# One exponential of a period among its transposes, routing and projection moved by half a pair

## The chip, the cores and the metric

One program runs on one core of a Trainium2 chip. The metric is the device time of a run in microseconds (us). The kernel before took 787.89 us in the median of three runs (787.39 to 789.18). The engines have short names throughout: PE is TensorE (matmul), PEld its weight load, DVE is VectorE, ACT is ScalarE, POOL is GpSimd, and SP is SyncE, which here only issues transfers (DMAs).

## The reference, cut to what matters

Attention over 4 batches of 8 heads, 768 tokens and 64 features, in which a query sees a key only if the signs of their projections on 6 vectors agree; then a top-1 mixture of 8 experts on the 3072 tokens.

```python
q_bits = (np.einsum('bhsd,dk->bhsk', q, proj) > 0).astype(np.int64)
k_bits = (np.einsum('bhsd,dk->bhsk', k, proj) > 0).astype(np.int64)
...
mask = q_bucket[:, :, :, None] == k_bucket[:, :, None, :]
scores = scale * np.matmul(q, k.transpose(0, 1, 3, 2))
scores = np.where(mask, scores, -1000000000.0)
scores = scores - np.max(scores, axis=-1, keepdims=True)
attn = np.exp(scores)
attn = attn / (np.sum(attn, axis=-1, keepdims=True) + 1e-09)
return np.matmul(attn, v).astype(np.float32)
...
logits = x @ w_gate
e_idx = np.argmax(logits, axis=1)
...
eom = 1.0 / (1.0 + np.exp(-(x @ w_output_gate)))
for e in range(E):
    mask = e_idx == e
    h = np.maximum(x[mask] @ w1[e], 0.0)
    out[mask] = gate_w[mask, None] * eom[mask, e, None] * (h @ w2[e])
```

## The kernel before

The first half of the program (to about 465 us) is the attention. It runs over 16 pairs of heads. A pair has 12 steps, one for each 128 queries of each of its two heads; 192 steps in all. Six steps are a period (`PER`), half a pair. Step s does this:

- PE makes the scores of step s (`scores`, line 529): for each half of the keys two matmuls, one with the rounded operands `xl`, `xr` and one with the remainders and the mask rows, `yl`, `yr`. The result has two PSUM buffers (`ps_s`). DVE takes the row minimum while it copies them out (line 533); only then is the PSUM buffer free.
- ACT makes the exponential (`soft`, line 541), DVE the reciprocal of two steps' sums (lines 548 and 549), POOL multiplies (`normal`, line 551).
- PE transposes the weights of step s-6 (`transposed`, line 562), in two halves of three, and ACT copies each half out (line 563). These also have two PSUM buffers (`ps_t`).

At the first step of a period (k == 0) PE also does the weighted sums of the half pair that was transposed in the period before (`weighted`, line 573, 24 matmuls with `ps_a`), between its score and its transposes. That is when ACT has no copies to make, and four exponentials stand there; the other two stand behind the transposes of the third and fourth step (k 2 and 3).

In every second period, the one that begins at step 12(g-1), the operands of pair g are made. I call it the operand period. POOL rounds q and k (`split_hi`, line 487), DVE makes the remainders (`split_lo`, line 495, four halves), PE projects q and k on the 6 vectors (`project`, line 407, behind the weighted sums), DVE turns the signs into mask rows (`bt`, line 410), and SP sends it all to its places with 16 DMAs (`spread`, lines 504 to 512). One of them copies `xl` inside itself and so waits for those that read the same rows; two write mask rows into `yl` and wait for the copy that reads `yl`. q and k of pair g are loaded by SP (`load`, line 394).

The order on PE, DVE, ACT and POOL is the order in which the program is written: the loop over the steps, with tables of functions by step (`at`, `first`, `amid`, `ahead`, `narrow`, `last`). The order on SP is set by a scheduler from when it expects things to be ready; SP then issues strictly in that order, and one that waits holds up all behind it.

When a batch of 4 pairs is through, its tokens are routed, in small pieces spread over the next batch's steps (`routing`). Counted from the first step of the next batch they stand at: router products at 6 and 12, `tokens` 8 and 14, `best` 15, `choose` 19, `prefix` and `ranks` 20, `gate_sums` 21, `gate_values` and `places` 22, `columns` 24, `hot` 25, `table` (12 matmuls, line 226) 28, `entries` 29. Nearly all of them are small DVE instructions. With three of the four batches routed, the first expert is picked (`pick`), its tokens gathered and its weights loaded and split, while the attention of the last batch still runs.

The second half of the program is the experts' matmuls, one expert after the other.

The structure that the change touches is this, at k == 0:

```python
elif k == 0:
    for fn in first.get(s, ()):
        fn()
    normals()
    softs(2)
    ...
if s >= PER and k in (2, 3):
    softs(1)
```

Of the kernel before, what the change touches and what calls it, by code (L numbers as in the profile page):

```python
# [19 lines left out]
B, H, S, D = 4, 8, 768, 64  # L20
NB = 6
P = 128
NT = S // P
# [36 lines left out]
def lsh_attention_then_moe(  # L60
# [307 lines left out]
    with ExitStack() as actx:  # L368
# [11 lines left out]
        at, first, amid, ahead, narrow, last = {}, {}, {}, {}, {}, {}  # L380
# [4 lines left out]
        def plan(step, *fns):  # L385
            at.setdefault(step, []).extend(fns)

# [329 lines left out]
        for g in range(NP):  # L717
            s0 = 12 * (g - 1)
            if g >= 2:
                plan(s0 - 8, lambda g=g: load(g))  # L720
                first.setdefault(s0, []).extend(lambda g=g, j=j: split_hi(g, j) for j in range(2))
                amid.setdefault(s0, []).extend(lambda g=g, n=n: split_lo(g, 0, n) for n in range(2))
                ahead.setdefault(s0, []).extend(lambda g=g, n=n: split_lo(g, 1, n) for n in range(2))
                narrow.setdefault(s0, []).append(lambda g=g: project(g))
                last.setdefault(s0, []).extend(lambda g=g, j=j: spread(g, j) for j in range(2))
            elif g == 1:
                plan(4, lambda: project(1))
                for j in range(2):
                    plan(2 + j, lambda j=j: split_hi(1, j))
                    for n in range(2):  # L730
                        plan(3 + 2 * j + n, lambda j=j, n=n: split_lo(1, j, n))
                    plan(5 + j, lambda j=j: spread(1, j))
            if g >= 1:
                plan(s0 + 10, lambda g=g: load_v(g))
            for hf in range(2 if g + 1 < NP else 1):
                narrow.setdefault(12 * g + 6 * hf + 2 * PER, []).extend(
                    lambda hb=2 * g + hf, c=c: weighted(hb, c) for c in range(NT))
                if g + 1 < NP:
                    plan(12 * g + 6 * hf + 2 * PER, lambda g=g, hf=hf: rows(g, hf))
        for i, fn in enumerate(more_constants()):  # L740
            plan(18 + 2 * i, fn)
        for b in range(B - 1):
            r = routing(b)
            s0 = 12 * (H // 2) * (b + 1)
            for hf in range(2):
                narrow.setdefault(s0 + PER * (hf + 1), []).insert(0, lambda r=r, hf=hf: r["logits"](hf, H // 2))
            for n, fn in ((8, lambda r=r: r["tokens"](0, H // 2)), (14, lambda r=r: r["tokens"](1, H // 2)),
                          (15, r["best"]), (19, r["choose"]), (20, r["prefix"]), (20, r["ranks"]),
                          (21, r["gate_sums"]), (22, r["gate_values"]), (22, r["places"]), (24, r["columns"]),
                          (25, r["hot"]), (28, r["table"]), (29, r["entries"])):  # L750
                plan(12 * (H // 2) * (b + 1) + n, fn)
# [4 lines left out]
        for hf in range(2):  # L756
            narrow.setdefault(s0 + PER * (hf + 1), []).insert(0, lambda hf=hf: r["logits"](hf, lp))
# [4 lines left out]
        late = 12 * (H // 2) * (B - 1) + 23  # L762
# [83 lines left out]
        with tc.manual_schedule(engines=MANUAL):  # L846
# [30 lines left out]

            for s in range(NSTEP + LAG):
# [13 lines left out]
                elif k == 0:  # L892
                    for fn in first.get(s, ()):
                        fn()
                    normals()
                    softs(2)
                    normals()
                    for fn in amid.get(s, ()):
                        fn()
                    softs(2)  # L900
                    normals()
                    for when in (ahead, narrow, last):
                        for fn in when.get(s, ()):
                            fn()
# [4 lines left out]
                if s >= PER and k in (2, 3):  # L909
                    softs(1)  # L910
# [257 lines left out]
```

## Time and profile before

| what | value |
|---|---|
| median of three runs | 787.89 us (787.39 to 789.18) |
| the profiled execution, its own time | 785.37 us |
| its span from the first to the last instruction | 783.7 us |
| PE busy | 753.6 us, 96% |
| PEld busy | 608.5 us, 78% |
| DVE busy | 494.7 us, 63% |
| ACT busy | 459.2 us, 59% |
| POOL busy | 389.9 us, 50% |
| mean granted clock of PE | 0.990 |

The shares are means over two halves that differ much: DVE, ACT and POOL have most of their work in the attention, where a period of six steps is the unit to look at. Matmuls are pipelined and their ends are modelled, so two of them can overlap in a timeline; distances between starts say more than lengths. A granted clock of 1.00 is 2.4 GHz, 0.50 is 1.2 GHz.

### The profile page before, as it was taken

Reading aid. Unit: us, or ns where it says so; the run is one execution under the profiler, and the core shown is the slowest. Engines: PE = TensorE matmul, PEld = TensorE weight load, DVE = VectorE, ACT = ScalarE, POOL = GpSimd, SP = SyncE. Lnnn points to the kernel's source line nnn. Section 1 sums busy time; section 2 is a strip of 40 time slices with the busy share of each in tenths; the row PEclk is TensorE's granted clock in tenths of the full one; section 3 lists DMA queues with packets and bytes.
Section 4 is the critical chain, followed back from the end, with each engine's and each line's share of the span. In section 5 each row is a group of like instructions: output and inputs, shape, how many; then the busy total and the mean of one; then the engine's idle time right before and its main releaser. Section 6 shows DMA issues by size and latency. Waiting matters only on the chain. (4 is left out here: it accounts for less than half of the span.)

```text
span 783.7 us, 13717 instructions
## 1 busy us (share of the span) xinstructions
PE 753.6 (96%) x4690; PEld 608.5 (78%) x4690; DVE 494.7 (63%) x1032; ACT 459.2 (59%) x934; POOL 389.9 (50%) x422
## 2 busy tenths in 40 slices
PE   6899999999999989999979999999999999999996
PEld 4676767667676767776756758888999999989895
DVE  5877877797786795787787727236263636454640
ACT  5787778876778767787857751234251525353331
POOL 7646553553555444556346873452527273646201
PEclk9999999999999989999999999999999999999999
DMA  5564565446456535465635331454444444446501
GB/s 168 123 147 95 111 148 119 108 114 139 87 126 147 122 83 120 89 146 130 139 75 160 77 91 41 143 193 139 145 149 153 151 152 150 148 154 214 196 17 39
DMA packets 84800, 98.90 MB, mean 126 GB/s; under 512 B 57999, under 2 KB 59439, under 8 KB 84720
## 3 DMA queue, kind: packets, MB, share of 16 engines
q1 hardware_dynamic: 79376, 84.58, 41.9%
q0 software_dynamic: 5200, 13.31, 5.2%
q8 instruction: 40, 0.66, 0.3%
q14 instruction: 40, 0.33, 0.1%
q10 hardware_dynamic: 144, 0.02, 0.0%
HBM read 59.49 MB, written 13.11 MB: 93 GB/s over the span
## 5 line engine op out<-in xcount | busy, mean ns | idle before, releaser
L551 POOL TENSOR_SCALAR sc<-sc,rsum 128x768 f32<-128x768 f32 x192 | 189.0, 998 | 206.0 <-DVE rsum L549 128.8
L533 DVE TENSOR_SCALAR_CACHE_REDUCE sc<-ps_s 128x768 f32<-128x768 f32 x192 | 182.4, 955 | 64.1 <-PE ps_s L529 54.5
L563 ACT COPY pts<-ps_t 128x384 f32<-128x384 f32 x384 | 165.5, 485 | 93.2 <-PE ps_t L562 93.2
L541 ACT ACTIVATE sc<-sc,mn 128x768 f32<-128x768 f32 x192 | 179.3, 940 | 19.5 <-DVE sc L533 18.4
L562 PE MATMUL ps_t<-ident,sc 128*128 128x128 f32 x1152 | 163.2, 278 | 5.9 <-POOL sc L551 1.7
L562 PEld LDWEIGHTS ps_t<-ident,sc 128*128 128x128 f32 x1152 | 132.8, 142 | 42.8 <-issue 20.2
L573 PE MATMUL ps_a<-pts,vt 128*64 128x384 f32 x768 | 131.1, 491 | 0.0
L529 PE MATMUL ps_s<-xr,xl 128*128 128x384 f32 x384 | 116.5, 385 | 14.7 <-DVE sc L533 12.4
L573 PEld LDWEIGHTS ps_a<-pts,vt 128*64 128x64 f32 x768 | 52.2, 137 | 67.8 <-issue 67.7
L323 DVE SCALAR_TENSOR_TENSOR hl<-ps_s,hh 128x256 fp32r<-128x256 f32 (+8 forms) x40 | 34.0, 850 | 108.4 <-ACT hh L322 87.1
L529 PE MATMUL ps_s<-yr,yl 76*128 76x384 f32 x384 | 100.6, 343 | 0.4 <-POOL yr L439 0.3
L312 PE MATMUL ps_s<-xh,w1h 128*128 128x256 f32 (+7 forms) x288 | 97.0, 337 | 0.0
L312 PE MATMUL ps_s<-xlo,w1h 128*128 128x256 f32 (+7 forms) x288 | 95.5, 331 | 0.0
L312 PE MATMUL ps_s<-xh,w1l 128*128 128x256 f32 (+7 forms) x288 | 95.4, 331 | 0.0
L286 POOL DMA_INDIRECT xq<-x_dram,idx x75 | 81.1, 1081 | 23.5 <-issue 21.0
L329 POOL DMA_INDIRECT out_dram<-yo,sid x29 | 31.2, 1076 | 121.3 <-ACT yo L328 77.6
L322 ACT ACTIVATE hh<-ps_s 128x256 fp32r<-128x256 f32 (+8 forms) x40 | 29.1, 726 | 98.1 <-PE ps_s L312 80.1
L529 PEld LDWEIGHTS ps_s<-xr,xl 128*128 128x128 f32 x384 | 59.5, 195 | 17.0 <-DVE sc L533 14.4
L529 PEld LDWEIGHTS ps_s<-yr,yl 76*128 76x128 f32 x384 | 71.3, 192 | 1.0 <-POOL yr L439 1.0
L495 DVE SCALAR_TENSOR_TENSOR yl<-qk,pj,xl 128x384 fp32r<-128x384 f32 x60 | 57.6, 997 | 2.1 <-POOL xl L487 1.8
L312 PEld LDWEIGHTS ps_s<-xh,w1h 128*128 128x128 f32 x288 | 54.2, 188 | 2.0 <-issue 0.6
L312 PEld LDWEIGHTS ps_s<-xh,w1l 128*128 128x128 f32 x288 | 54.2, 188 | 1.4 <-DVE w1l L178 0.3
(204 smaller groups left out, 1026.5 us busy)
## 6 DMA issues: line engine op xcount, KB each, us to landing
w_raw<-in_w_dram SPq DMA_DIRECT2D x36, 512.0 KB
qk<-in_qkT_dram SPq DMA_DIRECT2D x32, 384.0 KB
xh<-in_w_dram SPq DMA_DIRECT2D x14, 512.0 KB
xlo<-in_w_dram SPq DMA_DIRECT2D x14, 512.0 KB
vt<-in_v_dram SPq DMA_DIRECT2D x16, 384.0 KB
xr<-xl SPq DMA_DIRECT2D x30, 192.0 KB
yr<-xl SPq DMA_DIRECT2D x30, 192.0 KB
xr<-yl SPq DMA_DIRECT2D x30, 192.0 KB
```

What stands on the lines that cost most here:

```text
L286: nc.gpsimd.indirect_dma_start(out=xq[:, k * P:(k + 1) * P], out_offset=None, in_=x_dram.rearrange("n (a f) -> (n a) f", a=NB32), in_offse ...
L312: nc.tensor.matmul(ps, l, r, start=first and k == 0, stop=last and k == len(pairs) - 1)
L323: return lambda: nc.vector.scalar_tensor_tensor(hl, ph, 0.0, f32(hh), ALU.max, ALU.subtract)
L329: nc.gpsimd.indirect_dma_start(out=out[:, :], out_offset=bass.IndirectOffsetOnAxis(ap=sid[0:n, r, a:a + 1], axis=0), in_=yo[0:n], in_offse ...
L495: nc.vector.scalar_tensor_tensor(st["yl"][j][:, cs], st["qk"][j][:, cs], sgn, f32(st["xl"][j][:, cs]), ALU.mult, ALU.subtract)
L529: nc.tensor.matmul(ss[:, n, 0:HS], l[0:k, qs], r[0:k, n * HS:(n + 1) * HS], start=first, stop=not first)
L533: nc.vector.tensor_scalar(sc, ss[:, :, 0:HS], MASKED, None, ALU.min, ALU.min, accum_out=mn)
L541: nc.scalar.activation(pr, pr, AF.Exp, bias=mn, scale=-1.0, accum_out=sums[s // GROUP][:, k:k + 1])
L551: nc.gpsimd.tensor_scalar(live[s0 + k], live[s0 + k], rs[:, k:k + 1], 0.0, ALU.mult, ALU.add)
L562: nc.tensor.transpose(tr[:, c], pr[:, (3 * h + c) * P:(3 * h + c + 1) * P], ident)
L563: nc.scalar.copy(pts[:, 3 * h:3 * h + 3, t * P:(t + 1) * P], tr)
L573: nc.tensor.matmul(st["av"][j * D:(j + 1) * D], st["v"][:, j, c], blocks[hb][j][:, c], start=(c == 0), stop=(c == NT - 1))
```

## The change

Five tables of functions by step become one, `around`, with names for the places in the first step of a period. What moves:

- Exponentials: five of a period's six now stand at its first step, one of them behind the weighted sums in the program's order, and one behind the transposes of the third step.
- Projection: `project` of pair g moves from step 12(g-1) to 12(g-1)-6, the period before, behind its weighted sums. The load of q and k moves from 12(g-1)-8 to 12(g-1)-11.
- Remainders: the four pieces of `split_lo` stand one ahead of the first reciprocals, two behind them, and one behind the copy of the weighted sums.
- Routing: `choose` and `gate_sums` go to 18, `prefix` to 18, `gate_values` and `columns` to 30, `hot` to 31, `table` to 33 and `entries` to 34. Steps 18 to 23 and 30 to 35 are periods without operands. The work on the first expert (`late`) begins three steps later.

```diff
--- before.py
+++ after.py
@@ -377,13 +377,17 @@
         batches = [dict() for _ in range(B)]
         blocks = {}
         sums = {}
-        at, first, amid, ahead, narrow, last = {}, {}, {}, {}, {}, {}
+        at, around = {}, {}
 
 
         LAG = PER
 
         def plan(step, *fns):
             at.setdefault(step, []).extend(fns)
+
+        def block(step, when, *fns):
+
+            around.setdefault((step, when), []).extend(fns)
 
 
         def load(g, heads=(0, 1)):
@@ -717,12 +721,12 @@
         for g in range(NP):
             s0 = 12 * (g - 1)
             if g >= 2:
-                plan(s0 - 8, lambda g=g: load(g))
-                first.setdefault(s0, []).extend(lambda g=g, j=j: split_hi(g, j) for j in range(2))
-                amid.setdefault(s0, []).extend(lambda g=g, n=n: split_lo(g, 0, n) for n in range(2))
-                ahead.setdefault(s0, []).extend(lambda g=g, n=n: split_lo(g, 1, n) for n in range(2))
-                narrow.setdefault(s0, []).append(lambda g=g: project(g))
-                last.setdefault(s0, []).extend(lambda g=g, j=j: spread(g, j) for j in range(2))
+                plan(s0 - 11, lambda g=g: load(g))
+                block(s0 - PER, "matmuls", lambda g=g: project(g))
+                block(s0, "head", *(lambda g=g, j=j: split_hi(g, j) for j in range(2)))
+                block(s0, "early", lambda g=g: split_lo(g, 0, 0))
+                block(s0, "amid", lambda g=g: split_lo(g, 0, 1), lambda g=g: split_lo(g, 1, 0))
+                block(s0, "behind", lambda g=g: split_lo(g, 1, 1), *(lambda g=g, j=j: spread(g, j) for j in range(2)))
             elif g == 1:
                 plan(4, lambda: project(1))
                 for j in range(2):
@@ -733,8 +737,8 @@
             if g >= 1:
                 plan(s0 + 10, lambda g=g: load_v(g))
             for hf in range(2 if g + 1 < NP else 1):
-                narrow.setdefault(12 * g + 6 * hf + 2 * PER, []).extend(
-                    lambda hb=2 * g + hf, c=c: weighted(hb, c) for c in range(NT))
+                block(12 * g + 6 * hf + 2 * PER, "matmuls", *(
+                    lambda hb=2 * g + hf, c=c: weighted(hb, c) for c in range(NT)))
                 if g + 1 < NP:
                     plan(12 * g + 6 * hf + 2 * PER, lambda g=g, hf=hf: rows(g, hf))
         for i, fn in enumerate(more_constants()):
@@ -743,23 +747,24 @@
             r = routing(b)
             s0 = 12 * (H // 2) * (b + 1)
             for hf in range(2):
-                narrow.setdefault(s0 + PER * (hf + 1), []).insert(0, lambda r=r, hf=hf: r["logits"](hf, H // 2))
+                block(s0 + PER * (hf + 1), "logits", lambda r=r, hf=hf: r["logits"](hf, H // 2))
+            block(s0 + 3 * PER, "amid", r["choose"], r["gate_sums"])
+            block(s0 + 5 * PER, "amid", r["gate_values"], r["columns"])
             for n, fn in ((8, lambda r=r: r["tokens"](0, H // 2)), (14, lambda r=r: r["tokens"](1, H // 2)),
-                          (15, r["best"]), (19, r["choose"]), (20, r["prefix"]), (20, r["ranks"]),
-                          (21, r["gate_sums"]), (22, r["gate_values"]), (22, r["places"]), (24, r["columns"]),
-                          (25, r["hot"]), (28, r["table"]), (29, r["entries"])):
+                          (15, r["best"]), (18, r["prefix"]), (20, r["ranks"]), (22, r["places"]),
+                          (31, r["hot"]), (33, r["table"]), (34, r["entries"])):
                 plan(12 * (H // 2) * (b + 1) + n, fn)
 
         r = routing(B - 1)
         s0 = 12 * (NP - 1)
         lp = H // 2 - 1
         for hf in range(2):
-            narrow.setdefault(s0 + PER * (hf + 1), []).insert(0, lambda hf=hf: r["logits"](hf, lp))
+            block(s0 + PER * (hf + 1), "logits", lambda hf=hf: r["logits"](hf, lp))
             plan(s0 + PER * (hf + 1) + 2, lambda hf=hf: r["tokens"](hf, lp))
 
 
 
-        late = 12 * (H // 2) * (B - 1) + 23
+        late = 12 * (H // 2) * (B - 1) + 26
 
         def load_expert(idi, i):
             expert.append(nc.values_load(idi[0:1, i:i + 1], engines=(mybir.EngineType.SP,), min_val=0, max_val=E - 1))
@@ -875,6 +880,10 @@
                 while ready:
                     normal(ready.pop(0))
 
+            def now(when):
+                for fn in around.get((s, when), ()):
+                    fn()
+
             for s in range(NSTEP + LAG):
                 k = s % PER
                 if s < NSTEP:
@@ -890,23 +899,21 @@
                     normals()
                     softs(1)
                 elif k == 0:
-                    for fn in first.get(s, ()):
-                        fn()
+                    now("head")
+                    softs(2)
+                    now("early")
                     normals()
+                    now("amid")
                     softs(2)
                     normals()
-                    for fn in amid.get(s, ()):
-                        fn()
-                    softs(2)
-                    normals()
-                    for when in (ahead, narrow, last):
-                        for fn in when.get(s, ()):
-                            fn()
+                    for when in ("logits", "matmuls", "behind"):
+                        now(when)
+                    softs(1)
                 elif k == 3:
                     normals()
                 if s >= LAG:
                     transposed(s - LAG, live.pop(s - LAG))
-                if s >= PER and k in (2, 3):
+                if s >= PER and k == 2:
                     softs(1)
                 for fn in at.get(s, ()):
                     fn()
```

Lines behind the new function `block` have numbers four higher in the changed kernel (407 becomes 411). Three places show what the change does to the engines. The first is SP's queue at the end of the copies of pair 4, which are made in the period from step 36; `qk` with the next two numbers is q and k of pair 5. Before, with the projection of pair 5 at step 48:

```order
L507 DMA xl_1163<-xl_1163 64x768
L512 DMA yl_1182<-bt_1205 12x384
L511 DMA yr_1218<-bt_1205 12x384
L512 DMA yl_1182<-bt_1205 12x384
L394 DMA qk_1325<-in_qkT_dram 128x768
L394 DMA qk_1327<-in_qkT_dram 128x768
L592 DMA x_dram_63<-xb_1239 32x24x32 x4
L399 DMA vt_1479<-in_v_dram 128x768
```

and now, with the projection of pair 5 at step 42:

```order
L511 DMA xl_1168<-xl_1168 64x768
L516 DMA yl_1180<-bt_1027 12x384
L515 DMA yr_1216<-bt_1027 12x384
L516 DMA yl_1180<-bt_1027 12x384
L398 DMA qk_1264<-in_qkT_dram 128x768
L398 DMA qk_1266<-in_qkT_dram 128x768
L403 DMA vt_1484<-in_v_dram 128x768
L398 DMA qk_1605<-in_qkT_dram 128x768
```

The two loads stand behind the same copies as before, while their reader has moved six steps ahead. The same holds for both loads of pair 3 and for the second load of pairs 7, 9, 11, 13 and 15; the loads of pairs 4, 6, 8, 10, 12 and 14, and the first of those five, stand ahead of the copies or a period earlier.

The second is ACT in one period (`sc` the exponentials, `pts` the copies of transposes, two for a step). Before:

```order
L541 ACTIVATE sc,rsum<-sc,mn 128x768 x4
L563 COPY pts_1573<-ps_t 128x3x128 x2
L563 COPY pts_1574<-ps_t 128x3x128 x2
L563 COPY pts_1573<-ps_t 128x3x128 x2
L541 ACTIVATE sc,rsum<-sc,mn 128x768
L563 COPY pts_1574<-ps_t 128x3x128 x2
L541 ACTIVATE sc,rsum<-sc,mn 128x768
L563 COPY pts_1573<-ps_t 128x3x128 x2
L563 COPY pts_1574<-ps_t 128x3x128 x2
```

and now:

```order
L545 ACTIVATE sc,rsum<-sc,mn 128x768 x5
L567 COPY pts_1573<-ps_t 128x3x128 x2
L567 COPY pts_1574<-ps_t 128x3x128 x2
L567 COPY pts_1573<-ps_t 128x3x128 x2
L545 ACTIVATE sc,rsum<-sc,mn 128x768
L567 COPY pts_1574<-ps_t 128x3x128 x2
L567 COPY pts_1573<-ps_t 128x3x128 x2
L567 COPY pts_1574<-ps_t 128x3x128 x2
```

The exponential between the fourth and the fifth step's copies has gone to the group ahead of the first.

The third is DVE in the operand period from step 72, behind the copy of the weighted sums (`ot`), two periods after the first batch has ended (`bt` is the mask, `t_rhs` and `t_ob` the routing's columns and table, `sc,mn` the row minimum). Before:

```order
L495 SCALAR_TENSOR_TENSOR yl<-qk,pj,xl 128x384 x2
L576 COPY ot<-ps_a 128x384
L410 TENSOR_SCALAR bt<-ps_m,pj 128x384
L585 STREAM_TRANSPOSE xb<-ot 128x384
L211 TENSOR_TENSOR t_rhs<-oneh,t_oa 128x192
L215 TENSOR_TENSOR t_rhs<-t_rhs,toki 128x192
L215 TENSOR_TENSOR t_rhs<-t_rhs,gate 128x192
L533 TENSOR_SCALAR sc,mn<-ps_s 128x768
L220 TENSOR_TENSOR t_ob<-posi,t_pos 128x768
L533 TENSOR_SCALAR sc,mn<-ps_s 128x768 x2
```

and now, in the same period:

```order
L580 COPY ot<-ps_a 128x384
L499 SCALAR_TENSOR_TENSOR yl<-qk,pj,xl 128x384
L589 STREAM_TRANSPOSE xb<-ot 128x384
L537 TENSOR_SCALAR sc,mn<-ps_s 128x768 x3
L552 TENSOR_SCALAR rsum<-rsum 128x2
L553 RECIPROCAL rsum<-rsum 128x2
L537 TENSOR_SCALAR sc,mn<-ps_s 128x768 x3
```

The mask and four routing instructions are gone from there, and one remainder has come behind the copy; the routing instructions stand in the next period, where there are no remainders:

```order
L668 RECIPROCAL es<-es 128x6
L669 TENSOR_TENSOR gate<-den,es 128x6
L211 TENSOR_TENSOR t_rhs<-oneh,t_oa 128x192
L215 TENSOR_TENSOR t_rhs<-t_rhs,toki 128x192
L215 TENSOR_TENSOR t_rhs<-t_rhs,gate 128x192
L552 TENSOR_SCALAR rsum<-rsum 128x2
L553 RECIPROCAL rsum<-rsum 128x2
L580 COPY ot<-ps_a 128x384
L414 TENSOR_SCALAR bt<-ps_m,pj 128x384
L589 STREAM_TRANSPOSE xb<-ot 128x384
L537 TENSOR_SCALAR sc,mn<-ps_s 128x768
L220 TENSOR_TENSOR t_ob<-posi,t_pos 128x768
```

## Rows read from the trace of the kernel before

**Rows 1.** Busy time by stretch: start:end, us, each engine's busy us (instructions), clock, DMA.
```profile
211.15:223.93 12.78, 12.66 (x86) 9.38 (x85) 8.33 (x20) 10.46 (x25) 6.47 (x8) 1.00 0.76 172
85.60:99.17 13.57, 13.45 (x94) 9.53 (x93) 11.69 (x25) 10.46 (x25) 7.90 (x13) 1.00 0.44 93
139.87:153.72 13.85, 13.63 (x100) 9.93 (x96) 11.92 (x28) 10.31 (x27) 6.80 (x7) 1.00 0.51 106
166.79:184.80 18.01, 14.98 (x106) 11.07 (x105) 16.01 (x37) 10.86 (x25) 7.96 (x8) 1.00 0.42 88
278.77:299.30 20.53, 17.61 (x105) 13.82 (x104) 16.12 (x37) 11.10 (x25) 7.97 (x8) 0.83 0.41 84
393.27:413.57 20.30, 16.31 (x105) 12.39 (x105) 17.15 (x44) 10.87 (x25) 7.98 (x8) 0.92 0.40 83
```

**Rows 2.** Timeline of PE, long periods: start, us, operation, count [idle before, releaser].
```profile
178.10 0.62 PE L529 MATMUL ps_s<-xr,xl 128*128 128x384 f32 x2 [2.91 <-DVE sc L533]
...
181.31 1.48 PE L226 MATMUL ps_m<-t_rhs,t_ob 128*128 128x96 f32 x12
182.56 0.60 PE L529 MATMUL ps_s<-xr,xl 128*128 128x384 f32 x2
...
290.09 1.01 PE L529 MATMUL ps_s<-xr,xl 128*128 128x384 f32 x2 [2.92 <-DVE sc L533]
...
405.80 1.01 PE L529 MATMUL ps_s<-xr,xl 128*128 128x384 f32 x2 [3.99 <-DVE sc L533]
```

**Rows 3.** Timeline of PE, plain period from step 90: transposes of its last four steps.
```profile
217.94 0.82 PE L562 MATMUL ps_t<-ident,sc 128*128 128x128 f32 x6
...
219.30 0.82 PE L562 MATMUL ps_t<-ident,sc 128*128 128x128 f32 x6
...
220.77 0.85 PE L562 MATMUL ps_t<-ident,sc 128*128 128x128 f32 x6
...
222.44 0.85 PE L562 MATMUL ps_t<-ident,sc 128*128 128x128 f32 x6
```

**Rows 4.** Timeline of ACT, the same period.
```profile
215.75 0.86 ACT L563 COPY pts<-ps_t 128x384 f32<-128x384 f32 x2 [1.00 <-PE ps_t L562]
...
220.88 0.97 ACT L541 ACTIVATE sc<-sc,mn 128x768 f32<-128x768 f32 x1
```

**Rows 5.** Timeline of PE, operand period from step 36: the projection.
```profile
89.62 0.85 PE L407 MATMUL ps_m<-qk,pjc 128*32 128x384 f32 x8
```

**Rows 6.** Timeline of SP's queue, periods from steps 36 and 60.
```profile
88.81 0.46 SPq L506 DMA_DIRECT2D xr<-yl  x1
...
93.72 0.78 SPq L512 DMA_DIRECT2D yl<-bt  x1
...
97.33 0.59 SPq L506 DMA_DIRECT2D xr<-yl  x1
...
100.93 0.78 SPq L512 DMA_DIRECT2D yl<-bt  x1
...
103.34 0.99 SPq L394 DMA_DIRECT2D qk<-in_qkT_dram  x2
...
142.37 0.46 SPq L506 DMA_DIRECT2D xr<-yl  x1
```

**Rows 7.** Timeline of the start: the first loads and who waits for one.
```profile
0.80 1.82 SPq L394 DMA_DIRECT2D qk<-in_qkT_dram  x4
...
4.14 0.83 ACT L454 CAST xr<-qk 64x768 fp32r<-64x768 f32 x1 [1.62 <-DMA qk<-in_qkT_dram]
```

**Rows 8.** SP's queue from step 78, and stretches of 0.25 us (last: DMA share, GB/s).
```profile
186.93 0.98 SPq L394 DMA_DIRECT2D qk<-in_qkT_dram  x2
...
190.50:190.75 0.25, 0.25 (x5) 0.25 (x3) 0.22 (x1) 0.00 (x0) 0.00 (x0) 1.00 0.66 258
...
97.25:97.50 0.25, 0.25 (x2) 0.00 (x0) 0.00 (x0) 0.25 (x2) 0.25 (x1) 1.00 0.91 209
100.25:100.50 0.25, 0.25 (x4) 0.08 (x2) 0.22 (x4) 0.25 (x1) 0.00 (x0) 1.00 0.43 96
```

## The prediction

> **What bounds the kernel now.** I read the stretches first: the table of busy time by stretch, cut at the first weighted sum of a period [rows 1]. In the attention half, TensorE does nearly everything that takes time. A period without operand work (from step 90 here) lasts 12.78 us and PE is busy for 12.66 of them. A period in which the next pair's operands are made (from step 36) lasts 13.57, with 13.45 busy. The difference of 0.79 is the projection, which stands in the operand period. Neither waits for anything longer than a few tenths. What sticks out are the operand periods from steps 72, 120 and 168, the ones two periods behind a batch: 18.01, 20.53 and 20.30 us for the same matmuls. Together they are 58.84 - 3 x 13.57 = 18.1 us over an ordinary operand period. The timeline of PE [rows 2] shows why: at the fourth score of the period PE stands still 2.91, 2.92 and 3.99 us, each time for the row minimum on VectorE (L533), because there are two score buffers and DVE has not read the older one. DVE is the engine that is late: it has 8.3 us of work in a plain period and 11.7 in an operand period, and 16.0 to 17.2 in the three long ones [rows 1]. The routing work of the last batch (gate values, places, columns, the one-hot table) falls there.
>
> Two of the three gaps are followed by a lower granted clock (0.83 and 0.92 as the mean of the period [rows 1]); the pair of score matmuls behind the gap takes 1.01 us in place of 0.62 [rows 2], so this is TensorE at 1.2 GHz. After the gap of 2.91 us it did not fall, after the one of 2.92 it did. Its price, read from the periods: 20.53 - 18.01 = 2.5 us for the second, 20.30 - 18.01 - (3.99 - 2.91) = 1.2 for the third; I take 1.9.
>
> Then the timeline of PE and ACT inside the plain period. The transposes of two neighbouring steps should start 1.36 us apart; between the fifth and the sixth it is 1.67 [rows 3]. ACT explains it [rows 4]: the exponential at 220.88 stands ahead of the copies that free the transposes' PSUM buffers. Under the weighted sums, on the other hand, ACT is idle for 1.00 us before its first copy.
>
> **The exponentials.** The change takes the second exponential from among the transposes (1.67 becomes 1.36, so 0.31 us less a period) and sets it behind the four under the sums. There it takes 0.97 at most of the 1.00 us in which ACT is idle [rows 4]. Its cover is therefore complete but without reserve; in the periods that now hold the projection 0.79 more is free. 30 periods x 0.31 = 9.3 us less. Bounds: 0 (the fifth one delays the copies by as much as it saved) to 9.3. I take 9.3, since 1.00 is the nearest row.
>
> **The routing.** The three long periods hold 18.1 us too much, but the table's twelve matmuls (181.31 to 182.56, 1.25 us [rows 2]) move with it and stay on PE: 18.1 - 3 x 1.25 = 14.4 us can go, the clock's part included. DVE's surplus of 16.0 - 11.7 = 4.3 us per batch goes to periods without operands, where DVE is idle for 12.78 - 8.3 = 4.5; the mask of a projection, moved there too, eats some 0.6 of that. So most fits, but not all: the places still run in the last two steps ahead of the operand period, and the choice of the first expert, seven small DVE instructions, now stands inside the last operand period. What could come back is at most the surplus less the 13.57 - 11.7 = 1.9 us that such a period has free: 2.4 x 3 = 7.2 us. I take 2.0, near the lower end, because only one of the four groups remains there. Term: -12.4 us.
>
> **The projection.** It costs PE 0.79 us wherever it stands. DVE's wait for the mask vanishes from the queue of copies: the copy that needs the low half leaves at 88.81, and that of the mask into the same tile only 4.91 later, at 93.72 [rows 6]. But the projection now needs the pair's q and k six steps sooner. This is what I see against the change. The order of SP (shown above) still has the load of many pairs behind the sixteen copies that build the pair before it: both halves of pairs 3 and 5, the second half of pairs 7, 9, 11, 13 and 15. SP issues in order. So the question is when that queue is through, counted from the first weighted sum of the operand period (85.60 in the rows):
> - The copy that needs the low half leaves at 88.81, 3.2 after it; now a reciprocal stands between, 3.4.
> - The mask's copy into the same tile (93.72) must wait until that copy has landed. In the second head such a wait takes 100.93 - 97.33 = 3.60, with three 192 KB copies in one line whose bytes run from 97.25 to about 100.45, 1.07 us each, and 0.5 from the last byte to the release [rows 6, 8]. Alone, it costs between 1.07 + 0.5 = 1.6 and 3.60; I take the middle, 2.65.
> - From there to the load it is 103.34 - 93.72 = 9.62, all issue and waits between copies, which nothing in the change shortens.
> The load is issued 3.4 + 2.65 + 9.62 = 15.7 after the first sum, where it was 103.34 - 85.60 = 17.7. The first load of the kernel is issued at 0.80 and ACT starts on it at 4.14: 3.34 to land [rows 7]. Two in a row are issued at 186.93 and their bytes end at 190.75; with the 0.5 that is 4.3 [rows 8]. PE comes to the second half of the projection at 13.57 - 0.79 - 0.31 = 12.47 for the operand period, plus 4.02 for the sums (89.62 - 85.60 [rows 5]), plus half a projection: 16.9. In the periods from steps 60, 108 and 156 router work lengthens the stretch by 13.85 - 13.57 = 0.28 [rows 1] and the queue starts 3.21 - 2.50 = 0.7 sooner (142.37 - 139.87 [rows 6]).
> PE then stands for 15.7 + 3.34 - 16.9 = 2.1 us (pairs 9 and 13), 15.0 + 3.34 - 17.2 = 1.1 (pairs 7, 11, 15) and 15.7 + 4.3 - 16.9 = 3.1 (pairs 3 and 5): 4.2 + 3.3 + 6.2 = 13.7 us. With the bounds of the wait above: 6.4 to 20.4. The two gaps of 3.1 are as long as those behind which the clock fell in two of three cases: 2 x 1.9 = 3.8 us more; the shorter ones I leave without.
>
> The Trainium skill ("DMA: Bandwidth & Descriptors", section on the anatomy of one DMA) gives a fixed part of about 2.0 us and 436 GB/s, measured on the other issuing path: as an estimate 2.9 us for one such load and 3.8 for two. By it the waits would sum to 10.5 and the whole to 780.5; I keep the 3.34 of the row, since it is this load on this queue. The page also says that the semaphore fires only when the last byte is confirmed, which the 0.5 us between bytes and release bears out.
>
> **The sum.** -12.4 (routing) - 9.3 (exponentials) + 13.7 (loads) + 3.8 (clock) = -4.2 us. The profiled execution took 785.37 us, with a span of 783.7; its own sum is 781.2. The median of the runs is 787.89, 2.5 above it, so the runs should show 783.7. The experts' half is not touched: its first weights are loaded three steps later, but split and used in the same order, and the last split still ends ahead of the first product.
>
> **Rivals.**
> A. The loads land in time or nearly: the queue runs faster without the mask's wait, or the copies overlap better. For it speaks that DMA is busy for less than half of such a period (0.44 [rows 1]); against it that 9.62 us of the queue are untouched. Loads at 4 us, no clock: -12.4 - 9.3 + 4 = -17.7, 770.2 us. Chance 0.18.
> B, the other side. The queue of copies takes the place of the routing: PE waits for q and k in seven periods, the wait behind the low half's copy is 3.60 as in the second head (20.4 us), and the clock falls after the four gaps that are then 3 us or longer (4 x 1.9 = 7.6). -12.4 - 9.3 + 28.0 = +6.3, 794.2 us. It decides from the point at which loads and clock together cost more than the 21.7 us gained. For it: the only row for this wait is 3.60. Chance 0.20.
> C. The fifth exponential pushes the copies back in every period, since its cover has no reserve: the 9.3 are lost, +5.1, 793.0 us. Against it: half of the periods have 0.79 more. Chance 0.07.
> D. The change doesn't do what it says of the routing: the stall is not removed but split over more periods, with 7.2 given back in place of 2.0 and another fall of the clock of 1.5: +2.5, 790.4 us. Against it: DVE is free for 4.5 us there. Chance 0.08.
>
> **How the numbers follow.** My own case has 0.47, and 779 to 788 of its own. The range of 774 to 793 leaves out the far end of A and the end of B, about 2 in 10. Within 0.2% is 786.3 to 789.5, about what a measurement here can tell from no change. Own case: 0.37 faster, 0.08 same, 0.02 slower; A: all faster; B and C: 0.23 slower, 0.03 same, 0.01 faster; D: 0.04 slower, 0.04 same. Sum: faster 0.56, same 0.15, slower 0.29.
>
> **What would show it.** Right: no wait of PE for L533 above 1 us in the operand periods behind a batch, and a granted clock of 1.00 there; transposes 1.36 apart between fifth and sixth step; PE (or its weight load) waiting on the load of qk at the projection, in periods from steps 18, 42, 66, 90, 114, 138, 162, by 1 to 3 us. Wrong in the loads' step: no such wait (A), or waits of 3 to 4 us with the clock at half behind them (B). Wrong in the exponentials' step: ACT's first copy behind the sums starts later than 4.6 us after the first sum, and the first transposes spread. Wrong in the routing's step: PE still waits for L533, at steps 69 to 75 or 80 to 84.

## The result and the profile after

The changed kernel took 776.85 us in the median of four runs (774.56 to 777.66), the kernel before 788.02; the ratio is 0.9852, with an interval of 0.9828 to 0.9876. It is 11.2 us faster where 4.2 were forecast: the direction was right, the size was not. The profiled execution took 777.2 us (span 775.5, mean granted clock 0.994), against 785.37 (0.990) for that of before: 8.2 less.

The table of stretches, cut at the first weighted sums as in [rows 1] and with the same columns, of the changed kernel:

```profile
88.18:100.66 12.48, 12.48 (x86) 9.46 (x85) 10.34 (x24) 10.58 (x25) 7.98 (x13) 1.00 0.58 121
100.66:117.60 16.94, 14.15 (x94) 9.76 (x93) 8.70 (x21) 10.55 (x25) 6.14 (x7) 1.00 0.59 153
...
157.72:172.39 14.67, 14.47 (x100) 9.99 (x100) 11.59 (x36) 10.56 (x25) 5.69 (x7) 1.00 0.52 139
172.39:184.92 12.53, 12.53 (x86) 9.56 (x85) 11.46 (x27) 10.56 (x25) 7.76 (x8) 1.00 0.52 110
184.92:199.36 14.44, 14.44 (x105) 11.01 (x104) 11.55 (x31) 10.56 (x25) 7.30 (x8) 1.00 0.48 109
...
391.48:404.27 12.79, 12.79 (x85) 9.62 (x85) 12.32 (x34) 10.57 (x25) 7.75 (x8) 1.00 0.54 113
```

The fourth row is the operand period from step 72, 18.01 us before and now 12.53; the last is that from step 168, once 20.30. PE works through all of both, and VectorE has 11.5 and 12.3 us of work there in place of 16.0 and 17.2. The price stands in the second row, from step 42: a period with a projection and nothing else should last 12.48 + 0.79 = 13.27, and lasts 16.94. PE's timeline shows where (pair 3, then pair 5, then pair 9):

```profile
52.01 0.84 PE L411 MATMUL ps_m<-qk,pjc 128*32 128x384 f32 x4 [1.51 <-DMA qk<-in_qkT_dram]
53.26 0.84 PE L411 MATMUL ps_m<-qk,pjc 128*32 128x384 f32 x4 [0.41 <-DMA qk<-in_qkT_dram]
...
106.50 0.84 PE L411 MATMUL ps_m<-qk,pjc 128*32 128x384 f32 x4 [1.75 <-DMA qk<-in_qkT_dram]
108.38 0.84 PE L411 MATMUL ps_m<-qk,pjc 128*32 128x384 f32 x4 [1.04 <-DMA qk<-in_qkT_dram]
...
217.83 0.84 PE L411 MATMUL ps_m<-qk,pjc 128*32 128x384 f32 x4 [1.13 <-DMA qk<-in_qkT_dram]
```

Where two loads are late, PE waits, makes the first head's half, and waits again: no piece is longer than 1.75 us, and PE is idle for 1.51 + 0.41 = 1.92 us in pair 3 and 1.75 + 1.04 = 2.79 in pair 5. The rest of what these periods lose is not idle time: the eight matmuls of a whole projection take 0.85 us together [rows 5], the four of one head alone take 0.84, so a projection in two halves costs PE twice as much. The clock is 1.00 in all of these periods. SP's queue for pair 5, with the copies of pair 4 before it (in the form of [rows 6]; line 510 was 506, 516 was 512, 398 was 394):

```profile
90.91 0.46 SPq L510 DMA_DIRECT2D xr<-yl  x1
...
93.44 0.78 SPq L516 DMA_DIRECT2D yl<-bt  x1
...
103.07 0.98 SPq L398 DMA_DIRECT2D qk<-in_qkT_dram  x2
```

The two loads leave 103.07 - 88.18 = 14.89 us behind the first sum, where 15.7 was forecast. On ACT, the answer to [rows 4]: the fifth exponential of the period from step 36 and the first copy behind the sums,

```profile
91.70 0.93 ACT L545 ACTIVATE sc<-sc,mn 128x768 f32<-128x768 f32 x1
...
92.79 0.86 ACT L567 COPY pts<-ps_t 128x384 f32<-128x384 f32 x2
```

with next to no idle time left between them (in most of the 0.16 us ACT reads the accumulator of the exponential), and the copy no later behind the first sum (4.61 us) than in [rows 4] (215.75 - 211.15 = 4.60).

### The profile page after: what moved, and what is told of

Its sections match the earlier page's. It is cut to its first block, busy times and chain, and to the rows that moved or that the text cites. A ratio compares the mean times of both kernels' runs of the same rounds, so it can differ in the third digit from the quotient of the medians.

```text
span 775.5 us, 13677 instructions
## 1 busy us (share of the span) xinstructions
PE 750.9 (97%) x4690; PEld 607.9 (78%) x4690; DVE 483.2 (62%) x1032; ACT 460.9 (59%) x934; POOL 387.7 (50%) x422
## 5 line engine op out<-in xcount | busy, mean ns | idle before, releaser
L555 POOL TENSOR_SCALAR sc<-sc,rsum 128x768 f32<-128x768 f32 x192 | 185.9, 982 | 202.7 <-DVE rsum L553 99.4
L566 PE MATMUL ps_t<-ident,sc 128*128 128x128 f32 x1152 | 160.7, 275 | 3.3 <-ACT pts L567 2.9
L286 POOL DMA_INDIRECT xq<-x_dram,idx x75 | 82.7, 1102 | 23.7 <-issue 20.8
L312 PEld LDWEIGHTS ps_s<-xlo,w1h 128*128 128x128 f32 x288 | 54.2, 188 | 1.3 <-DVE xlo L269 0.2
```

Source lines behind the costliest of these rows:

```text
L286: nc.gpsimd.indirect_dma_start(out=xq[:, k * P:(k + 1) * P], out_offset=None, in_=x_dram.rearrange("n (a f) -> (n a) f", a=NB32), in_offse ...
L312: nc.tensor.matmul(ps, l, r, start=first and k == 0, stop=last and k == len(pairs) - 1)
L555: nc.gpsimd.tensor_scalar(live[s0 + k], live[s0 + k], rs[:, k:k + 1], 0.0, ALU.mult, ALU.add)
L566: nc.tensor.transpose(tr[:, c], pr[:, (3 * h + c) * P:(3 * h + c + 1) * P], ident)
```

## The experiments

In the traces I compare the length from the first weighted sum (step 12) to the last (step 198), which leaves out the start and the experts: 432.88 us in the profiled execution of before, 423.04 after.

**before_again**: the kernel before, unchanged.

> The kernel before, unchanged, to see how its own executions differ. Theory 1 (the fall of the clock behind the three long gaps differs from run to run): the runs lie between 785 and 789.5 us, and time and mean granted clock go together, at about 784 x 0.001 = 0.8 us for each 0.001 of clock; the profiled execution of 785.37 at 0.990 was one with only two falls, runs at 788 show 0.986 to 0.988. Theory 2 (the 2.5 us between the profiled execution and the median have nothing to do with the clock): runs at 788 show 0.990 too.

Twelve runs of it had 787.63 to 790.16 us at clocks of 0.980 to 0.984; the runs of before beside them had 788.11 to 794.40 at 0.977 to 0.986. So the execution on which the forecast rests, 785.37 at 0.990, was better than all of these, and theory 2 is out. Theory 1 holds in its kind, but its 0.8 us for each 0.001 of clock does not show from run to run: 787.65 us had 0.982, 790.14 had 0.984. The three long periods of its trace (columns as in [rows 1]):

```profile
168.39:189.01 20.62, 17.66 (x105) 13.88 (x104) 16.15 (x37) 11.12 (x25) 8.03 (x8) 0.83 0.40 84
282.98:302.26 19.28, 16.35 (x105) 12.61 (x105) 16.06 (x37) 11.11 (x25) 8.00 (x8) 0.91 0.43 88
396.24:417.89 21.65, 17.65 (x106) 13.64 (x105) 17.17 (x44) 11.09 (x25) 8.01 (x8) 0.84 0.38 80
```

Here the clock fell behind all three gaps; the first period takes 20.62 in place of 18.01. The three together take 61.55 us against 58.84, and the stretch 435.69 against 432.88: nearly the whole difference lies in them. Of the 4.6 us between the two spans (788.3 and 783.7) 2.7 are theirs and 1.6 the start's, whose first sum comes at 34.49 in place of 32.91.

**only_routing**: before, with the routing's pieces and the first expert's work moved, nothing else.

```diff
-  (15, best), (19, choose), (20, prefix), (20, ranks), (21, gate_sums), (22, gate_values), ...
+  amid at s0 + 18: choose, gate_sums;  amid at s0 + 30: gate_values, columns
+  (15, best), (18, prefix), (20, ranks), (22, places), (31, hot), (33, table), (34, entries)
-late = 12 * (H // 2) * (B - 1) + 23
+late = 12 * (H // 2) * (B - 1) + 26
```

> The kernel before, with the routing's pieces (and the work on the first expert) moved as in the changed kernel, nothing else. Theory 1: the three long periods of 18.0 to 20.5 us become 13.6, the table's 1.25 goes to the next period: 14.0 us less by the profile, and since no gap is left behind which the clock can fall, the run-to-run part of 2.5 us goes too: 771.5 to 774, mean clock 0.994 or above. Rival (the stall is only spread): 4 to 8 us less, with waits of PE for the row minimum in the plain periods that now hold the routing.

Measured 775.02 us against 789.18, ratio 0.9806 (0.9780 to 0.9832): alone it gains what the whole change does, or more. Theory 1 holds in its mechanism: 14.2 us less, at the small end of its 14.0 to 16.5. Clocks of 0.989 to 0.992 are a little under what I expected; in the trace the clock is 0.50 from 19.7 to 30.0 us, in the start, and 1.00 from there to the end of the attention. The periods from steps 72 and 78:

```profile
168.66:182.67 14.01, 13.51 (x93) 9.63 (x93) 12.77 (x28) 10.59 (x25) 7.70 (x8) 1.00 0.40 84
182.67:196.34 13.67, 13.67 (x98) 10.87 (x97) 11.07 (x30) 10.58 (x25) 7.33 (x8) 1.00 0.70 158
```

0.44 us is left of the stall (0.47 and 0.56 in the other two long periods); the stretch is 418.71, 14.2 less than the profiled execution of before and 17.0 less than the trace of before_again. The rest of the change costs more than it gives: 423.04 - 418.71 = 4.3 us.

**early_loads**: the changed kernel, with one number changed.

```diff
-plan(s0 - 11, lambda g=g: load(g))
+plan(max(1, s0 - 14), lambda g=g: load(g))
```

> The changed kernel with q and k of a pair asked for 14 steps ahead in place of 11, by which each load stands ahead of the sixteen copies of the pair before in SP's order. Theory 1 (PE's waits for q and k in seven periods are the whole of the loads' cost, 14.0 us by the lengths of the periods): 776.9 - 14.0 = 762.9 us, no wait of PE for a load at the projection. Rival (the loads then collide with the copies, or the projection waits for something else that is late too): 766 to 772.

Measured 765.83 us, ratio 0.9686 (0.9661 to 0.9712): the fastest version here, 3.1% under before. In SP's order both loads of a pair now stand directly ahead of the copies of the pair before, and no wait of PE for a load is left. The periods from steps 24 and 42:

```profile
61.10:73.58 12.48, 12.48 (x86) 9.46 (x85) 10.38 (x24) 10.58 (x25) 8.62 (x14) 1.00 0.59 125
...
99.30:112.54 13.24, 13.24 (x93) 9.61 (x93) 8.69 (x21) 10.55 (x25) 6.14 (x7) 1.00 0.55 135
```

13.24 against 16.94 for step 42. The stretch is 410.33, so the late loads cost 423.04 - 410.33 = 12.7 us. The medians give 11.0, with different runs of before beside them. Theory 1 holds in its mechanism, with 11 to 12.7 us where it had 14.0.

**only_projection** and **only_projection_early**: before, with the projection half a pair up, and the loads at 11 or at 14 steps.

```diff
-plan(s0 - 8, lambda g=g: load(g))
+plan(s0 - 11, lambda g=g: load(g))            # in the second: max(1, s0 - 14)
-narrow.setdefault(s0, []).append(lambda g=g: project(g))
+narrow.setdefault(s0 - PER, []).append(lambda g=g: project(g))
```

> The kernel before with the projection half a pair sooner and q and k asked for 11 steps ahead, as in the changed kernel; exponentials, remainders and routing stay. Theory 1 (the loads' wait is a cost of this move alone, 12.7 us by the periods of the changed kernel against those with early loads): PE waits at the projection in seven or eight periods, 10 to 14 us, the three long gaps stay: 789.1 + 12 = 801 us. Rival (in the queue of the kernel before there is room, and the waits of the changed kernel come from PE being faster): less than 4 us, 793 at most.

> The same with q and k asked for 14 steps ahead, so that every load stands ahead of the copies of the pair before. Theory 1 (a projection costs PE 0.79 us wherever it stands, and alone it gains nothing): 789 us, within 2. Rival (the mask's 0.66 us gone from VectorE's queue shortens the three long gaps by as much each, and the clock falls less): 784 to 786.

Measured 798.48 (ratio 1.0107, 1.0077 to 1.0136) and 788.24 (0.9983, 0.9968 to 0.9998): the move alone makes the kernel slower, by its loads; with the loads in time it is worth next to nothing. Theory 1 in both, with an error in the first: against the second the late loads cost 798.48 - 788.24 = 10.2 us, at the lower end, and by the lengths of the periods PE waits for them in five (from steps 18, 42, 66, 102 and 150), not in seven or eight. The waits of only_projection for pairs 3 and 5 are worth a look:

```profile
52.87 0.84 PE L407 MATMUL ps_m<-qk,pjc 128*32 128x384 f32 x4 [1.56 <-DMA qk<-in_qkT_dram]
54.56 0.84 PE L407 MATMUL ps_m<-qk,pjc 128*32 128x384 f32 x4 [0.85 <-DMA qk<-in_qkT_dram]
...
109.17 1.87 PE L407 MATMUL ps_m<-qk,pjc 128*32 128x384 f32 x8 [1.86 <-DMA qk<-in_qkT_dram]
```

Behind 1.56 the four products take 0.84 us, behind 1.86 the eight take 1.87 where 0.85 is usual [rows 5]: here the clock did fall, behind a piece only a tenth of a microsecond longer than the longest of the changed kernel (the granted clock from 108 to 118 us is 0.83).

**only_exponentials**: before, with five exponentials at the first step and one among the transposes.

```diff
 for when in (ahead, narrow, last): ...
+softs(1)
-if s >= PER and k in (2, 3):
+if s >= PER and k == 2:
```

> The kernel before, with five exponentials at a period's first step and one among the transposes, nothing else moved. Theory 1 (it is worth 0.31 us in each of 30 periods and adds up with the other parts): 9.3 us less, some 778.7 against 788.0, transposes of fifth and sixth step 1.36 apart. Rival (in the kernel before, where the mask stands in the queue of DVE behind the sums, the fifth exponential has no cover and only the whole change makes it pay): 0 to 3 us less, ACT's first copy behind the sums later.

Measured 785.79, ratio 0.9962 (0.9943 to 0.9981), 3.4 us less: the rival's size, but not by its mechanism. Plain periods go from 12.78 to 12.46; ordinary operand periods become longer, 13.77 for 13.57. ACT is idle for 0.86 us ahead of its first copy there, so the exponential has its cover. The loss is on VectorE (its queue behind the sums, then PE's wait):

```profile
89.32 2.08 DVE L495 SCALAR_TENSOR_TENSOR yl<-qk,pj,xl 128x384 fp32r<-128x384 f32 x2
91.32 0.55 DVE L576 COPY ot<-ps_a 128x384 f32<-128x384 f32 x1
91.79 0.66 DVE L410 TENSOR_SCALAR bt<-ps_m,pj 128x384 fp32r<-128x384 f32 x1
92.37 0.56 DVE L585 STREAM_TRANSPOSE xb<-ot 128x384 f32<-128x384 f32 x1
92.87 0.91 DVE L533 TENSOR_SCALAR_CACHE_REDUCE sc<-ps_s 128x768 f32<-128x768 f32 x1
```

```profile
93.85 0.61 PE L529 MATMUL ps_s<-xr,xl 128*128 128x384 f32 x2 [0.39 <-DVE sc L533]
```

The row minimum stands behind two remainders and the mask, and as soon as PE is quicker it is late.

**exponentials_back** and **remainders_back**: the kernel with early loads, with one part undone.

```diff
 for when in ("logits", "matmuls", "behind"): now(when)     # exponentials_back
-softs(1)
-if s >= PER and k == 2:
+if s >= PER and k in (2, 3):
```

```diff
-block(s0, "early", split_lo 0,0); block(s0, "amid", split_lo 0,1 and 1,0); block(s0, "behind", split_lo 1,1)
+block(s0, "amid", split_lo 0,0 and 0,1); block(s0, "logits", split_lo 1,0 and 1,1)     # remainders_back
```

> The kernel with early loads (765.8 us), with the exponentials put back as in the kernel before: four at a period's first step, two among the transposes. Theory 1 (the exponentials are worth 0.31 us a period once the mask is out of the operand period): 31 x 0.31 = 9.6 us more, 775.4. Rival (what only_exponentials showed, 3.4 us, is all they are worth): 769.

> The kernel with early loads (765.8 us), with the four remainders of a pair put back where they stood, two behind the first reciprocals and two behind the second, all ahead of the copy of the sums. In only_exponentials the operand periods lost 0.39 us to a row minimum that was late behind two remainders (2.08 us) and the mask (0.66). Theory 1 (the mask's departure is the cover that the exponentials need): the mask's 0.66 is more than the 0.39, so operand periods stay at 12.5 and the time within 1 us of 765.8. Rival (the new places of the remainders are the cover): some 0.4 us in each of 14 operand periods, 771.4.

exponentials_back: 772.58 (ratio 0.9787, 0.9773 to 0.9801), a stretch of 416.86: the exponentials are worth 416.86 - 410.33 = 6.5 us in the kernel with early loads, between the two expectations. In most periods they give 0.3; in those from steps 54, 102, 150 and 186 they give about 0.16, and in those that hold a projection beside the table (14.46 with them, 14.45 without) or beside other routing products (14.00, 13.99) they give nothing. Why not, I did not test.

remainders_back: 775.01 (ratio 0.9825, 0.9812 to 0.9839), 9 us more. My theory fell and its rival holds, with a higher price than its 0.4 us a period: ordinary operand periods take 13.2 to 13.3 for 12.48, with a wait like this one in eight of them and one of 1.1 us in the three behind a batch (those from steps 60, 108 and 156 have none and are as long as before):

```profile
95.09 0.62 PE L533 MATMUL ps_s<-xr,xl 128*128 128x384 f32 x2 [0.66 <-DVE sc L537]
```

I had reckoned with the mask's 0.66 us off VectorE, and not with the projection's 0.79 off PE in the same period: PE comes sooner by more than VectorE does. By these figures the wait would be 0.39 + 0.79 - 0.66 = 0.52, and it is 0.66. One remainder in VectorE's idle time ahead of the first reciprocals and one behind the copy of the sums are what makes room.

**wide_gaps**: the changed kernel, with longer waits in one piece.

```diff
-block(s0 - PER, "matmuls", lambda g=g: project(g))
+block(s0 - PER, "matmuls")
+around[(s0 - PER, "matmuls")].insert(NT // 2, lambda g=g: project(g))
 def project(g):
-    for j in range(2):
+    for j in (1, 0):
```

> The changed kernel with the projection in the middle of the weighted sums, 2.05 us sooner, and the second head's half first, so that PE waits for both loads in one piece. By SP's order only the loads of pairs 3, 5, 9 and 13 are then late: one piece of some 4.9 and three of some 4.0 us in the places of the waits of the changed kernel. Theory 1 (the clock falls behind an idle piece of PE of 3 us and more, whoever it waits for; in the changed kernel it did not fall since its waits came in pieces of 1.8 us at most): the clock is at half behind all four, 2 to 2.6 us for each, 765.8 + 16.8 + 9 = 791.6 us. Rival (the falls in the kernel before belong to something else in its long periods, VectorE's work for example): no fall, 782.6 us.

Measured 795.28, ratio 1.0074 (1.0053 to 1.0095). PE's waits, and the clock in the ten microseconds around each (the third figure from the end):

```profile
54.63 1.51 PE L411 MATMUL ps_m<-qk,pjc 128*32 128x384 f32 x8 [6.82 <-DMA qk<-in_qkT_dram]
...
113.28 1.51 PE L411 MATMUL ps_m<-qk,pjc 128*32 128x384 f32 x8 [3.95 <-DMA qk<-in_qkT_dram]
...
143.72 0.85 PE L411 MATMUL ps_m<-qk,pjc 128*32 128x384 f32 x8 [1.09 <-ACT lt L613]
```

```profile
54.00:64.00 10.00, 9.37 (x47) 5.27 (x48) 3.29 (x6) 1.99 (x5) 0.00 (x0) 0.66 0.44 125
112.00:122.00 10.00, 8.72 (x44) 4.62 (x45) 2.92 (x6) 1.72 (x4) 1.55 (x2) 0.66 0.43 141
143.00:153.00 10.00, 9.28 (x70) 7.20 (x70) 6.26 (x15) 5.92 (x16) 2.88 (x4) 1.00 0.63 160
```

The other two long waits (4.09 and 3.87) show 0.83 and 0.67. The clock falls behind all four that wait for a load, so VectorE's work is not what it takes; behind the three pieces of 1.09 it does not fall. The first piece was longer than the 4.9 expected. The four make 18.7 us. The price of a fall is what such a period lasts beyond the same period of early_loads, less the wait: from step 18, 23.22 - 13.24 - 6.82 = 3.2 us, and in the same way 2.9, 1.8 and 2.9 for the others. That is 10.7 us, 2.7 each, where I had put 2 to 2.6. The stretch is 443.19 - 410.33 = 32.9 us longer; the 3.4 that are left come mostly from the waits of 1.09 for ACT, which the move of the projection brings with it. The traced execution was the slowest of four, 798.35.

The test varies two things at once: these waits are in one piece, and they are longer than the 1.92 and 2.79 us of idle time in the changed kernel. Which of the two counts is for the next run to say.

**idle_alone**: the disputed cost by itself.

> Leaves out the whole computation, and its output is zeros: TensorE alone, products of 128x384 without a break, interrupted by idle pieces in which VectorE works on the last product, of eight lengths (about 1 to 6 us) and three kinds of two pieces with five products between them, each kind six times. Theory 1 (the length of the piece decides): the granted clock stays at 1.00 behind pieces up to about 2 us, is sometimes at 0.50 behind pieces of about 3 and always behind pieces of 4 and more; two pieces with products between them count as each alone. Rival (the sum of the idle time counts): two pieces of 2 us each behave as one of 4.

The cost of a fall is the time from the end of a piece to the fortieth PE instruction behind it, less the 12.97 us that this takes where the clock did not fall:

| idle piece, us | falls, of six | cost of a fall, us |
|---|---|---|
| 1.14 and 1.53 | 0 each | - |
| 1.93 and 2.32 | 4 each | 1.7 |
| 2.72 | 4 | 1.5 to 1.7 |
| 3.11 | 4 | 1.5 to 1.7, once 3.1 |
| 3.90 | 6 | 1.5 to 1.7 (three), 2.7 to 3.1 (three) |
| 5.09 | 6 | 2.1 to 2.8 |

For an example, the products behind pieces of 1.53 and 3.90 us, two each in four instructions:

```profile
223.38 1.53 PE L88 MATMUL ps<-t,wt 128*128 128x384 f32 x4 [1.53 <-DVE t L96]
...
820.74 2.90 PE L88 MATMUL ps<-t,wt 128*128 128x384 f32 x4 [3.90 <-DVE t L96]
```

The same four instructions take 1.53 us in the first and 2.90 in the second (that the first has 1.53 twice is chance). In two pieces with five products between, 1.93 and 1.04 us fell in two cases of six and 1.93 and 1.83 in three, each time behind the first piece; a sum of 3.76 would have fallen always, if sums counted as one piece of 3.90 does. Two pieces of 2.72 and 2.62 fell in five cases of six, behind the first in four and behind the second in two (one case fell twice), where one piece of 5.09 fell always. So the piece counts, as far as six cases of a kind can say; that a piece shortly before makes no difference at all, they cannot say. All first or single pieces of 1.93 together fell in nine cases of eighteen. My bound of 2 us for the harmless ones was a little high.

## Why the forecast was wrong

By the prediction's own steps, with the stretch of the attention:

- **The exponentials** (-9.3) **and the projection's cost of nothing.** Together 418.71 - 410.33 = 8.4 us less, from only_routing to early_loads; 6.5 of it are the exponentials, so rival C is out. The transposes of the fifth and sixth step are now 1.39 apart (97.81 and 99.20 in the period from step 36), for 1.67. What I got wrong is the cover: I looked for it on ACT, where it was complete, and the place that could have lost it was VectorE's queue in front of the row minimum. The new places of the remainders saved it, 9 us that the forecast never priced.
- **The routing** (-12.4). It gained 14.2 (only_routing against the execution that I reckoned with). I had 2.0 come back; in the changed kernel it is 0.06, 0.06 and 0.31 in the three operand periods, 0.4 in all, with no wait of PE for the row minimum of 0.1 us or more there. In only_routing, where the mask and the remainders still stand there, it is 1.5. Rival D is out.
- **The loads** (+13.7). 12.7 us, in just the seven periods named, from 0.7 (pair 7) to 3.7 us (pair 5). The copy that needs the low half left 2.73 us behind the first sum, for 3.4; the mask's wait was 93.44 - 90.91 = 2.53, for 2.65; from there to the load it was 9.63, for 9.62. So close a sum is luck, since three errors offset each other. The loads left sooner than forecast, by 0.6 to 0.8 us in six periods and 0.1 in that of pair 15, 4.5 us in all. Landing took 1.3 us more in all, 1.0 of it in pair 5 (PE goes on at 108.38, 5.3 us behind 103.07, for 4.3), where a load of v and two more of q and k followed within 2.6 us; in pair 3, where only that of v followed in that time, it was 53.26 - 48.90 = 4.4. And I counted the half of a projection behind a late load as half of 0.85 us, where it takes 0.84: 0.42 in each of the seven periods, 2.9 in all, that the forecast put at nothing. The 0.7 that these leave over lie in the three periods with router products (pairs 7, 11 and 15). Of the 12.7, PE is idle for 7.8. A late load alone, that of pair 9, was issued at 214.35 and PE goes on at 217.83: 3.5 us, close to the 3.34 of [rows 7]. The estimate from the Trainium skill ("DMA: Bandwidth & Descriptors", the anatomy of one DMA) was 2.9 for it; the trace is above that. Rival A, that they land in time, is out.
- **The clock** (+3.8). This step failed. I reasoned that two gaps of 3.1 us are as long as those behind which the clock fell. The two periods lost 2.8 and 3.7 us, but PE's idle time in them was 1.92 and 2.79, in two pieces of at most 1.75 with the first head's products between, and nothing fell: 0. That fits idle_alone, where pieces of 1.53 never fell and those of 1.93 in half of the cases; that it was the break, and not the smaller idle time, rests on that bench and not on a run of this kernel.
- **From the profiled execution to the runs** (+2.5). This failed too. I took the distance between the median of before and its profiled execution as fixed. That execution was an uncommonly good one: it is faster than each of the 34 timed runs of the same program in the rounds of before_again. The one slower execution with a trace lies 4.6 us above it, and 2.7 of that is the clock behind the three routing gaps; where no gap is, as in only_routing, this part is gone. The four runs behind the median of 788.02 have no trace, so how much of their 2.65 was the gaps stays open. After the change the median is 0.35 us *under* the profiled execution.

With the measured terms, -14.2 - 8.4 + 12.7 + 0 = -9.9, and the stretch shows 423.04 - 432.88 = -9.8. The start took 1.0 us more (33.94 for 32.91) and what follows the last sum 0.7: with these it is -8.2, the difference of the profiled executions. The remaining 3.0 to -11.2 are the 2.65 by which the median of before lay above its profiled execution (788.02 - 785.37) and the 0.35. So of the 7.0 us by which the forecast was off, 3.8 stand in the one step and 3.0 in the other; the errors of the other terms (-1.8, +0.9 and -1.0) and the +1.7 of the start and the end cancel to 0.2, by chance.

Rival B had the mask's wait too long (3.60, where 2.53 was measured) and let the clock fall, which it did not; wide_gaps, with four waits of 3.9 to 6.8 us, is about what it described, and came to its side of before. Left open: whether the clock falls in some executions of the changed kernel behind its 1.75 us, since only one of them has a trace (clocks of 0.992 to 0.997 leave little room), and what the falls in the start, which differ between executions, follow.

## What to carry to other kernels

When an operation is moved up, look for what it reads in the order of the queue that brings it: here one number that puts two loads ahead of sixteen copies was worth more than the exponentials. Price a wait of TensorE by its unbroken pieces as well as by its sum, ask whether an operation that is split still runs its parts side by side, and reckon a kernel with gaps from the clocks of several executions, not from one profile. Where PE gets quicker, check the queue of every engine that PE waits for, not only the one that took on the work.

## What the hardware showed beyond that

A gap of PE need not be long to cost more than itself: in idle_alone the clock never fell behind 1.53 us, behind 1.93 in nine cases of eighteen, and a fall took another 1.5 to 3.1 us. The same program ran at mean clocks of 0.977 to 0.990 with nothing changed, 785.4 to 794.4 us; of the 4.6 us between two of its traces more than half came from three gaps of 3 to 4 us. Eight matmuls of the form 128*32 took 0.85 us together and four of them 0.84. Two loads of 384 KB released PE 4.4 us after their issue where one more load followed closely, and 5.3 where three did; whether those were the cause, no run tests.
